# Two blocks of key weights loaded together through GpSimd's queue, with a new order of the head, in a two-layer linear-attention and MLP kernel

## The chip, the cores and the metric

The kernel runs on one core of one Trainium2 chip. The core has five engines that run side by side, each through its own list of instructions, in order: TensorE (PE, matrix products; PEld is its weight loads), VectorE (DVE), ScalarE (ACT), GpSimd (POOL) and SyncE (SP). SP, ACT and POOL can also issue DMAs; all DMAs run on the core's 16 DMA engines. The metric is the device time of one execution in microseconds. Times inside the profile count from the start of the profiled span.

## What is computed

`x` is 2048 tokens of 512 numbers in bf16. Two kinds of blocks alternate, A, B, A, B, each behind a layer norm and with a residual:

```python
def _A_ref(x, wqkv, wo):
    qkv = (x @ wqkv).reshape(B, S, 3, H, Dh)...      # H = 32, Dh = 16
    phi = lambda t: jnp.where(t > 0, t + 1, jnp.exp(t)) + 1e-6
    pq, pk = phi(q), phi(k)
    kv = jnp.einsum("bhsd,bhse->bhde", pk, v)
    z = jnp.einsum("bhsd->bhd", pk)
    num = jnp.einsum("bhqd,bhde->bhqe", pq, kv)
    den = jnp.einsum("bhqd,bhd->bhq", pq, z)[..., None] + 1e-6
    return (num / den)... @ wo

def _B_ref(x, w1, b1, w2, b2):
    y = _layernorm(x, axis=-1)
    h = _gelu(jnp.einsum("bsd,df->bsf", y, w1) + b1)                 # F = 1792
    return jnp.einsum("bsf,fd->bsd", h, w2) + b2

x = x + _A_ref(_layernorm(x, axis=-1), A_wqkv, A_wo)
x = x + _B_ref(_layernorm(x, axis=-1), B_w1, B_b1, B_w2, B_b2)
x = x + _A_ref(_layernorm(x, axis=-1), A_wqkv, A_wo)
x = x + _B_ref(_layernorm(x, axis=-1), B_w1, B_b1, B_w2, B_b2)
```

Linear attention needs the sum over all tokens of `pk` times `v` before any output: a first pass over the tokens builds that sum, a second one uses it.

## The kernel before, in words

**Tiles.** The tokens are cut into four chunks of 512 (c = 0 to 3) and each chunk into four row tiles of 128 (st = 4c + k). The 512 features are four blocks of 128. Weights stay in the on-chip memory once loaded: `wqkv` (queries, keys, values side by side, four feature blocks each), `wo`, `w1`, `w2`.

**The first pass (the head).** For each row tile of the first block A: statistics of the layer norm on VectorE (statsA0_st, aggrA0_st, L775 and L777), the reciprocal root on GpSimd (vepsA0_st at L782, powA0_st at L784), the normed row tile (normA0_st, L803 on VectorE or L798 on ScalarE), a transpose (TA0_st), the key product (K0_st, L879: one matmul for each of the four feature blocks), the key's `phi` (expk0_st at L847, reluk0_st at L858, mink0_st and phik0_st on VectorE, L860 and L864), and the product that sums `pk` times the normed tile over all row tiles (G0_st, L984, held in four PSUM banks). The sum of `pk` (Z0_c, L970) and the queries (Q0_c_k, L896 and L909) run in between. Values are never formed for each token: the sum is multiplied with the value weights at the end (KV0, L1034).

The first tiles take short cuts. Row tiles 0 and 1 are only centred (cenA0_st, L789), transposed on PE (PTC0, PTC1 at L825, brought back by ACT as tcC0, tcC1 at L835), and scaled later, inside the exponential and the relu of their keys. Tiles 2 and 3 are normed and transposed on PE too (PTA0_2, PTA0_3, tcA0_2, tcA0_3). Tile 3's statistics are made by ACT (sumA0_3 at L766, sqA0_3 at L770, with negA0_3 on GpSimd between them). All other transposes are DMAs on SP's queue (L812). The key product of tile 0 is cut into parts, so that each waits only for the key blocks it reads: `"ks0": "2|0|3|1"` makes four parts of one matmul (K0_0a to K0_0d), which read blocks 2, 0, 3 and 1 in that order.

Before that work, while nothing has been loaded, PE runs 15 matmuls on a constant whose result nobody reads (warm0 to warm8, L749).

**The loads at the start.** `LOADS` (L243) lists them: name, queue, what, chunk or 0, first and last block, and what must be done first. x0 is the first row tile of chunk 0, x1 the other three, xc1 to xc3 the other chunks of `x` (512 KB each), wq the query weights (512 KB), and wka, wkb, wkc, wkd one key block each (128 KB). SP issues x0, x1, wka, wkc, then xc1 (which waits until x0 has landed), wq, xc3, and later xc2 among its transposes; ACT issues wkb (behind `ones`, a VectorE memset) and wkd. The remaining weights (wv, wo, w1, w2) are issued by GpSimd much later, at L728, when all first transposes are issued.

GpSimd starts with small constants: id0 and id1 (the unit matrix `idp`, L719 and L720, read by the PE transposes), neghalf (L722), and bdm0 and bdm1 (the block-diagonal mask, L731 and L734, the first of which needs `ones`).

**The order.** The program is built as a graph of named operations. Nothing is scheduled at run time or at build time: `ORDER` holds the full list of operations of each engine, written out, and `PLACES` the buffer each tile lives in. `Settled.run` (L144) takes the lists as they are, and `assign_waits` (L186) puts the semaphore waits that the graph needs before each operation. So an operation that waits holds up all that stand behind it on its engine.

**The rest.** After KV0 and the products M0, the second pass makes outputs of block A (WO0, L1123), the MLP (W10 at L1153, gelu at L1158, W20 at L1190) and, chunk by chunk, the first pass of the next block A. The last layer writes the output from L1202 and L1184.

Of the kernel before, what the change touches and what calls it, by code (L numbers as in the profile page):

```python
# [185 lines left out]
def assign_waits(graph, order, sems, dma_sems):  # L186
# [1173 lines left out]
```

## Time and profile before

| What | us |
|---|---|
| median of 3 runs | 323.23 (323.01 to 323.62) |
| the profiled execution | 323.1, with a span of 321.9 |
| first matmul of useful work (PTC0) | starts 4.61 |
| x0 lands | 3.23 |
| xc1 issued, landed | 3.24, 8.07 |
| PE's last idle time over 0.1 us before the tail (0.47) | ends 9.16 |
| PE busy | 318.0 of 321.9 |
| last matmuls (L1176) | 316.70 to 319.92 |

In the views of the trace that follow, a row of the chain in order of time has a start, a length and what ran. A row of the timeline has a start, a length, the engine, the line of the kernel, the operation, what it writes and reads with sizes, and in brackets how long its engine had been idle before it and what ended that. Lengths of PE rows are a little longer than what they hold back, since matmuls overlap: eight 512-column matmuls that start 0.216 us apart show as 1.89 us on the timeline. The granted clock of the core was 1.00.

### The profile page before, as it was taken

To read this page: it belongs to the slowest core of one execution; us is meant where nothing else is said; L and a number is where in the kernel's file an instruction comes from. 1 tells how busy PE (TensorE), PEld (TensorE's weight loads), DVE (VectorE), ACT (ScalarE), POOL (GpSimd) and SP (SyncE) were. 2 spreads that over 40 slices of the span, in tenths; PEclk is the share of its full clock that TensorE was granted. 3 is DMA by queue.
4 is the path that set the end of the run, shared out by engine and by line. 5 is a ranking of instruction groups with operands and counts; after the bars stand their busy time and mean duration, and the time that the engine had idled before them with its cause. 6 is when DMAs were issued, how large, how long until landed. Compare 5 with 4: busy or idle time off the path is not lost.

```text
span 321.9 us, 4748 instructions
## 1 busy us (share of the span) xinstructions
PE 318.0 (99%) x1703; PEld 157.4 (49%) x1703; DVE 218.1 (68%) x529; ACT 189.3 (59%) x324; POOL 145.5 (45%) x216
## 2 busy tenths in 40 slices
PE   8999999999999999999999999999999999999997
PEld 3444554666444444444444444558544444444444
DVE  5998789999786774028848899999889881101103
ACT  5898656797730636667962367979634442663320
POOL 6573978688655355101822415887454163000000
DMA  7844793142121412111010200122232322201002
GB/s 257 200 81 85 241 348 85 35 82 36 33 49 34 82 33 51 34 33 32 18 40 10 51 16 0 35 51 52 50 62 54 98 65 67 49 0 35 16 33 65
DMA packets 52355, 21.68 MB, mean 67 GB/s; under 512 B 47532, under 2 KB 50860, under 8 KB 52332
## 3 DMA queue, kind: packets, MB, share of 16 engines
q1 hardware_dynamic: 50844, 16.37, 22.4%
q0 software_dynamic: 1056, 4.72, 4.3%
q10 hardware_dynamic: 432, 0.30, 0.3%
q8 instruction: 13, 0.21, 0.3%
q14 instruction: 10, 0.08, 0.1%
HBM read 8.00 MB, written 2.10 MB: 31 GB/s over the span
## 4 chain that ended last, share of the span: by engine, by line
PE 97%; DMA 2%; DVE 0%; issue 0%
PE ps L1153 30%; PE ps L1190 29%; PE ps L1123 9%; PE ps L879 8%; PE ps L896 6%; PE ps L984 4%; PE ps L1013 4%; DMA t<-in_A_x_dram 2%; PE ps L909 2%; PE ps L1176 1%; PE ps L970 1%; PE ps L1034 1%; PE ps L1057 1%; PE ps L1100 1%; DVE stats L775 0%; PE ps L1048 0%
## 5 line engine op out<-in xcount | busy, mean ns | idle before, releaser
L1158 ACT ACTIVATE gT<-ps,b1c 128x512 bf16<-128x512 f32 (+1 forms) x140 | 77.0, 601 | 68.7 <-PE ps L1153 68.1
L1153 PE MATMUL ps<-t,w 128*128 128x512 bf16 (+1 forms) x560 | 102.5, 336 | 0.0
L1190 PE MATMUL ps<-w,gT 128*128 128x512 bf16 x434 | 98.6, 379 | 0.0
L1153 PEld LDWEIGHTS ps<-t,w 128*128 128x128 bf16 x560 | 54.8, 98 | 43.7 <-ACT gT L1158 0.2
L1190 PEld LDWEIGHTS ps<-w,gT 128*128 128x128 bf16 x434 | 42.5, 98 | 50.4
L784 POOL TENSOR_TENSOR rstd<-veps,neghalf 128x1 f32<-128x1 f32 x64 | 39.0, 625 | 41.1 <-DVE veps L782 38.9
L847 ACT ACTIVATE eb<-ps 128x512 bf16<-128x512 f32 x62 | 35.4, 606 | 19.3 <-PE ps L896 7.3
L1200 DVE TENSOR_TENSOR yb<-ps,xsb 128x512 bf16<-128x512 f32 x15 | 10.2, 688 | 41.4 <-PE ps L1190 41.4
L775 DVE BATCH_NORM_STATS2 stats<-xsb 128x6 f32<-128x512 f32 x48 | 32.0, 681 | 0.3
L1123 PE MATMUL ps<-gtb,t 128*128 128x512 bf16 x128 | 31.4, 379 | 0.0
L879 PE MATMUL ps<-wqkv,t 128*128 128x512 bf16 x128 | 30.9, 379 | 0.3 <-ACT t L835 0.3
L858 ACT ACTIVATE rb<-ps 128x512 bf16<-128x512 f32 x43 | 25.3, 607 | 5.8 <-PE ps L879 5.8
L798 ACT ACTIVATE yb<-xsb,nmr,rstd 128x512 bf16<-128x512 f32 x21 | 16.9, 814 | 15.1 <-POOL nmr L795 15.1
L896 PE MATMUL ps<-wqkv,t 128*128 128x512 bf16 x96 | 24.1, 379 | 0.0
L1089 POOL TENSOR_TENSOR t<-t,rr 128x512 bf16<-128x512 bf16 x18 | 19.3, 1072 | 9.0 <-DVE rr L1085 6.4
L782 POOL TENSOR_SCALAR veps<-mv 128x1 f32<-128x1 f32 x35 | 8.2, 236 | 32.7 <-DVE mv L777 31.3
L1196 DVE TENSOR_TENSOR xsb<-ps,xsb 128x512 f32<-128x512 f32 x16 | 10.8, 678 | 17.9 <-PE ps L1190 17.9
L1139 POOL TENSOR_TENSOR xsb<-xsb,b2b 128x512 f32<-128x512 f32 x17 | 21.4, 1267 | 3.0 <-DVE yb L803 2.9
L1077 POOL TENSOR_TENSOR lr<-t,zrow 128x512 f32<-128x512 bf16 x14 | 16.5, 1179 | 7.3 <-ACT zrow L997 4.5
L1123 PEld LDWEIGHTS ps<-gtb,t 128*128 128x128 bf16 x128 | 12.5, 98 | 14.5
L803 DVE TENSOR_SCALAR yb<-xsb,mv,rstd 128x512 bf16<-128x512 f32 x27 | 14.5, 542 | 7.3 <-POOL rstd L784 6.0
L879 PEld LDWEIGHTS ps<-wqkv,t 128*128 128x128 bf16 x128 | 12.1, 98 | 14.7 <-ACT t L835 0.9
(99 smaller groups left out, 363.7 us busy)
## 6 DMA issues: line engine op xcount, KB each, us to landing
w<-in_B_w_dram POOLq DMA_DIRECT2D x4, 896.0 KB, 9.1
out_dram<-yb SPq DMA_DIRECT2D x15, 128.0 KB, 2.0
t<-in_A_x_dram SPq DMA_DIRECT2D x3, 512.0 KB, 4.8
t<-yb SPq DMA_TRANSPOSE x62, 2.5
wqkv<-in_A_wqkv_dram SPq DMA_DIRECT2D x1, 512.0 KB, 5.9
wqkv<-in_A_wqkv_dram POOLq DMA_DIRECT2D x1, 512.0 KB, 4.7
wo<-in_A_wo_dram POOLq DMA_DIRECT2D x1, 512.0 KB, 5.3
t<-in_A_x_dram SPq DMA_DIRECT2D x1, 384.0 KB, 3.3
```

Source lines behind the costliest of these rows:

```text
L775: G.op("dve", lambda e: e.bn_stats(stats[:, s.slot, :], src()), 620, reads=src_keys, writes=[k + "s"], tiles=[s, *src_tiles], name=f"stats ...
L784: G.op("pool", lambda e: e.tensor_tensor(rstd[:, s.slot:s.slot + 1], veps[:, s.slot:s.slot + 1], neghalf[:], op=ALU.pow), 570, reads=[k + ...
L847: G.op("act", lambda e: e.activation(eb[:, et.slot, :], bank(bt), ACT.Exp, scale=by()), 478, reads=[src_key, *more_keys], writes=[f"e{tag} ...
L858: G.op("act", lambda e: e.activation(rb[:, rt.slot, :], bank(bt), ACT.Relu, scale=by()), 478, reads=[src_key, *more_keys], writes=[f"r{tag ...
L879: ins = e.matmul(bank(b), lhsT=yTa(yT)[:, dt, k * P:(k + 1) * P], rhs=wqkv[:, dt, D:2 * D], start=(i == 0 and n == 0), stop=(i == len(part ...
L896: ins = e.matmul(bank(b), lhsT=yTa(yT)[:, dt, k * P:(k + 1) * P], rhs=wqkv[:, dt, 0:D], start=(dt == 0), stop=(dt == DT - 1))
L1089: lambda e, d=d, tok=tok, heads=heads: e.tensor_tensor(heads(tok()), heads(tok()), rr[:, d.slot, :].unsqueeze(2).broadcast_to([P, H, DH]), ...
L1123: ins = e.matmul(bank(wb), lhsT=yTa(pq)[:, kt, k * P:(k + 1) * P], rhs=gtb[:, kt, :], start=(kt == 0), stop=(kt == DT - 1))
L1139: G.op("pool" if on_pool else "dve", lambda e: e.tensor_tensor(xsb[:, st, :], xsb[:, st, :], b2b[:], op=ALU.add), 1120 if on_pool else 600 ...
L1153: ins = e.matmul(bank(b, n), lhsT=w1[:, dt, ft * P:(ft + 1) * P], rhs=yTa(yT)[:, dt, k0 * P:k1 * P], start=(dt == 0), stop=(dt == DT - 1))
L1158: G.op("act", lambda e, ft=ft, b=b, k0=k0, k1=k1, n=n: e.activation(gT[:, g.slot, ft * 512 + k0 * P:ft * 512 + k1 * P], bank(b, n), ACT.Ge ...
L1190: ins = e.matmul(bank(b), lhsT=gT[:, g.slot, ft * 512 + k * P:ft * 512 + (k + 1) * P], rhs=w2[:, ft, :], start=(ft == 0), stop=(ft == FT - 1))
```

## The change

Five things change in the tables, and several functions get options that this kernel's tables leave unused.

1. Key blocks 2 and 3 came by ACT's queue (wkb, wkd), blocks 0 and 1 by SP's (wka, wkc). Now blocks 2 and 3 come together in one load of 256 KB, wkp, issued by GpSimd; ACT's wkb carries block 0 and SP's wka block 1, and wkc and wkd no longer exist.
2. GpSimd's list starts id0, neghalf, id1, bdm0, bdm1, wkp instead of id0, neghalf, bdm0, bdm1, id1; wkp waits for nothing but its turn.
3. The key product of tile 0 is cut into three parts, block 0, block 1, and blocks 2 and 3 together. K0_0d no longer exists; K0_0c has two matmuls and waits for wkp.
4. The orders of all five engines in the head (and, with small differences, on to the second pass) and the places of many tiles are new. G0_0 now stands ahead of K0_3 on PE. On VectorE, mink0_0 moves ahead of normA0_1, and normA0_5 moves behind phik0_1. On GpSimd wv, wo and w1 move apart, with phik0_8 between wv and wo and phiq0_1_1 between wo and w1. One of the warm matmul groups moves from behind PTC0 to ahead of it.
5. A few operations change their engine: pr0_3_1, pr0_3_3, b20_2 and nine of the small veps operations swap between VectorE and GpSimd.

```diff
-    LOADS=[['x0', 'sp', 'x', 0, 0, 1, ''], ['x1', 'sp', 'x', 0, 1, 4, ''], ['wkb', 'act', 'wk', 0, 2, 3, 'ones'], ['wka', 'sp', 'wk', 0, 0, 1, ''], ['wkd', 'act', 'wk', 0, 3, 4, ''], ['wkc', 'sp', 'wk', 0, 1, 2, ''], ['xc1', 'sp', 'x', 1, 0, 4, 'x0'], ['wq', 'sp', 'wq', 0, 0, 4, ''], ['xc3', 'sp', 'x', 3, 0, 4, ''], ['xc2', 'sp', 'x', 2, 0, 4, '']],
+    LOADS=[['x0', 'sp', 'x', 0, 0, 1, ''], ['x1', 'sp', 'x', 0, 1, 4, ''], ['wkb', 'act', 'wk', 0, 0, 1, 'ones'], ['wka', 'sp', 'wk', 0, 1, 2, ''], ['wkp', 'pool', 'wk', 0, 2, 4, ''], ['xc1', 'sp', 'x', 1, 0, 4, 'x0'], ['wq', 'sp', 'wq', 0, 0, 4, ''], ['xc3', 'sp', 'x', 3, 0, 4, ''], ['xc2', 'sp', 'x', 2, 0, 4, '']],
+    CHUNKS=[[0, 1, 2, 3], [0, 1, 2, 3], [0, 1, 2, 3]],
...
         "sp":
-            "x0 x1 wka wkc xc1 wq xc3 TA0_0 TA0_1 xc2 TA0_5 TA0_4 TA0_7 TA0_6 TA0_13 TA0_14 TA0_15 TA0_12 TA0_8 TA0_10 TA0_9 "
+            "x0 x1 wka xc1 wq xc3 TA0_0 TA0_1 xc2 TA0_5 TA0_4 TA0_7 TA0_6 TA0_13 TA0_14 TA0_12 TA0_8 TA0_15 TA0_10 TA0_9 "
...
         "pe":
-            "warm0 warm8 warm2 warm6 PTC0 warm1 warm7 warm5 warm4 warm3 K0_0a K0_0b PTC1 K0_0c K0_0d PTA0_2 K0_1 PTA0_3 K0_2 "
-            "K0_3 G0_0_0 G0_1_0 Q0_0_2 Q0_0_1 Q0_0_0 K0_5 G0_2_0 K0_4 Z0_0 G0_3_0 Q0_1_0 K0_7 Q0_1_3 K0_6 G0_4_0 G0_5_0 "
+            "warm0 warm1 warm6 warm8 warm4 PTC0 warm2 warm5 warm7 K0_0a warm3 K0_0b PTC1 K0_0c PTA0_2 K0_1 PTA0_3 K0_2 G0_0_0 "
+            "K0_3 G0_1_0 Q0_0_1 Q0_0_2 Q0_0_0 K0_5 G0_2_0 Q0_1_0 K0_4 K0_7 G0_3_0 Q0_1_3 G0_4_0 Z0_0 K0_6 Q0_1_2 G0_5_0 K0_14 "
...
         "act":
-            "wkb wkd sumA0_3 tcC0 sqA0_3 tcC1 reluk0_0 tcA0_2 expk0_0 tcA0_3 expk0_1 reluk0_1 reluk0_3 expk0_2 reluk0_2 "
+            "wkb sumA0_3 tcC0 sqA0_3 tcC1 expk0_0 tcA0_2 reluk0_0 expk0_1 tcA0_3 reluk0_1 expk0_2 reluk0_3 reluk0_2 expk0_3 "
...
         "dve":
-            "ones statsA0_0 aggrA0_0 cenA0_0 statsA0_2 statsA0_1 aggrA0_2 aggrA0_1 cenA0_1 normA0_0 vepsA0_1 normA0_2 "
-            "statsA0_5 normA0_3 aggrA0_5 normA0_1 statsA0_4 mink0_0 aggrA0_4 phik0_0 mink0_1 normA0_5 phik0_1 statsA0_7 "
+            "ones statsA0_0 aggrA0_0 cenA0_0 statsA0_2 statsA0_1 aggrA0_2 aggrA0_1 cenA0_1 normA0_0 normA0_2 vepsA0_1 "
+            "statsA0_5 normA0_3 mink0_0 normA0_1 phik0_0 aggrA0_5 statsA0_4 mink0_1 aggrA0_4 phik0_1 normA0_5 statsA0_7 "
...
         "pool":
-            "id0 neghalf bdm0 bdm1 id1 vepsA0_0 powA0_0 negA0_3 vepsA0_2 powA0_2 vepsA0_3 powA0_3 powA0_1 vepsA0_5 powA0_5 "
...
-            "nmrA0_10 vepsA0_9 powA0_9 nmrA0_11 phik0_14 eps6 wv wo phik0_8 w1_0 w1_1 w2_0 w2_1 phiq0_1_1 pr0_0_0 pz0_1_0 "
+            "id0 neghalf id1 bdm0 bdm1 wkp vepsA0_0 powA0_0 negA0_3 vepsA0_2 powA0_2 vepsA0_3 powA0_3 powA0_1 b1z vepsA0_5 "
...
+            "vepsA0_10 powA0_10 vepsA0_9 nmrA0_10 nmrA0_11 powA0_9 phik0_14 wv phik0_8 wo phiq0_1_1 w1_0 w1_1 w2_0 w2_1 "
...
-        "den0_3": "tok", "den1_1": "tok", "den1_2": "tok", "den1_3": "tok", "ks0": "2|0|3|1", "normA0_0": "dve",
+        "den0_3": "tok", "den1_1": "tok", "den1_2": "tok", "den1_3": "tok", "ks0": "0|1|23", "normA0_0": "dve",
```

The options that stay unused are a load of half a row tile (`load_half`), queries of half a chunk in the other layout (`by_half`), and another order of the chunks: `CHUNKS` keeps 0, 1, 2, 3 in each pass, so `attn_z`, `attn_g_held`, `attn_g_chunk`, `attn_out` and `mlp_up` build the same operations as before with a flag for the first or last chunk in place of a comparison with 0 or 3.

More of the change, by code (lines that the diff above doesn't have):

```diff
@@ L709, in load_w, with load_half @@
                                [f"{which}_{d}" for d in range(d0, d1)], name=name, kb=128 * (d1 - d0), after=after)
+        def load_half(name, queue, h, after):
+            G.parts[("x0", 0)] = (("x0", 0, 0), ("x0", 0, 1))
+            ps_ = slice(64 * h, 64 * h + 64)
+            loaded[name] = dma(queue, lambda e: e.dma_start(
+                t4[ps_, x0[0].slot, 0:D].rearrange("p (k d) -> p k d", k=1), rows(x_dram, 0)[ps_, 0:1, :]),
+                [("x0", 0, h)], [x0[0]], name=name, kb=64, after=after)
         for name, queue, what, at, lo, hi, behind in cf["LOADS"]:
             after = [loaded[b] for b in behind.split()]
-            if what == "x":
+            if what == "half":
+                load_half(name, queue, at, after)
+            elif what == "x":
                 load_x(name, queue, at, lo, hi, after)
@@ L751, in build_kernel, with by_token, by_half @@
             G.op("pe", warm, sum(cols) / 1.2, tiles=[wu], name=f"warm{n}", n=len(cols))
-        def by_token(L, c):
-            return eng(f"den{L}_{c}") == "tok"
+        def by_token(L, c, k=0):
+            way = eng(f"den{L}_{c}")
+            return way == "tok" or (way == "half" and k >= 2)
+        def by_half(L, c):
+            return eng(f"den{L}_{c}") == "half"
+        tokq = {}
         def norm(src, src_keys, src_tiles, double, on_act, tag, src16=False, head=False, centred=None):
@@ L854, in phi @@
                                                              op0=ALU.add, op1=ALU.max),
-                     600, reads=[f"e{tag}", src_key], writes=[dst_key], tiles=[et, bt, *dst_tiles], name=f"phi{tag}", lat=90)
+                     600 if n == D else 330, reads=[f"e{tag}", src_key], writes=[dst_key], tiles=[et, bt, *dst_tiles], name=f"phi{tag}", lat=90)
                 return
             rt = Tile(RB, f"r{tag}")
-            G.op("act", lambda e: e.activation(rb[:, rt.slot, :], bank(bt), ACT.Relu, scale=by()), 478, reads=[src_key, *more_keys],
+            G.op("act", lambda e: e.activation(rb[:, rt.slot, 0:n], bank(bt, n), ACT.Relu, scale=by()), 478 if n == D else 265, reads=[src_key, *more_keys],
@@ L887, in attn_q, with fn @@
         def attn_q(L, c, yT, pq):
-            if by_token(L, c):
-                for k in range(4):
+            half = by_half(L, c)
+            own = pq
+            if half:
+                own = tokq[(L, c)] = Tile(T4, f"pqt{L}_{c}")
+            n = 2 * P if half else 4 * P
+            if not by_token(L, c):
+                for kt in range(DT):
+                    b = Tile(psum, f"q{L}_{c}_{kt}" + "c" * half, "q")
+                    def fn(e, kt=kt, b=b):
+                        for dt in range(DT):
+                            ins = e.matmul(bank(b, n), lhsT=wqkv[:, dt, kt * P:(kt + 1) * P], rhs=yTa(yT)[:, dt, 0:n],
+                                           start=(dt == 0), stop=(dt == DT - 1))
+                        return ins
+                    G.op("pe", fn, 4 * MM if n == D else 4 * (n / 2.4 + 2.5), reads=[f"yT{L}_{4 * c + k}" for k in range(n // P)] + ["wq"], writes=[f"q{L}_{c}_{kt}" + "c" * half],
+                         tiles=[b, yT], name=f"Q{L}_{c}_{kt}" + "c" * half, lat=MM_DRAIN, n=4)
+                    phi(b, f"q{L}_{c}_{kt}" + "c" * half, lambda kt=kt: yTa(pq)[:, kt, 0:n], f"pq{L}_{c}_{kt}" + "c" * half, [pq], f"q{L}_{c}_{kt}" + "c" * half, n=n)
+            for k in range(4):
+                if by_token(L, c, k):
                     b = Tile(psum, f"q{L}_{c}_{k}", "q")
@@ L900, in attn_q, with attn_z @@
                          tiles=[b, yT], name=f"Q{L}_{c}_{k}", lat=MM_DRAIN, n=4)
-                    phi(b, f"q{L}_{c}_{k}", lambda k=k: t4[:, pq.slot, k * D:(k + 1) * D], f"pq{L}_{c}_{k}", [pq],
+                    phi(b, f"q{L}_{c}_{k}", lambda k=k: t4[:, own.slot, k * D:(k + 1) * D], f"pq{L}_{c}_{k}", [own],
                         f"q{L}_{c}_{k}")
-                return
-            for kt in range(DT):
-                b = Tile(psum, f"q{L}_{c}_{kt}", "q")
-                def fn(e, kt=kt, b=b):
-                    for dt in range(DT):
-                        ins = e.matmul(bank(b), lhsT=wqkv[:, dt, kt * P:(kt + 1) * P], rhs=yTa(yT)[:, dt, :],
-                                       start=(dt == 0), stop=(dt == DT - 1))
-                    return ins
-                G.op("pe", fn, 4 * MM, reads=[f"yT{L}_{4 * c + k}" for k in range(4)] + ["wq"], writes=[f"q{L}_{c}_{kt}"],
-                     tiles=[b, yT], name=f"Q{L}_{c}_{kt}", lat=MM_DRAIN, n=4)
-                phi(b, f"q{L}_{c}_{kt}", lambda kt=kt: yTa(pq)[:, kt, :], f"pq{L}_{c}_{kt}", [pq], f"q{L}_{c}_{kt}")
         zfirst = {}
-        def attn_z(L, c, pks):
-            by_sum = [int(v) for v in (eng("zc0") or "").split()] if L == 0 else list(range(NC - 1))
+        def attn_z(L, c, pks, order):
+            by_sum = [int(v) for v in (eng("zc0") or "").split()] if L == 0 else order[:NC - 1]
+            others = [v for v in order if v not in by_sum]
             def fold(add):
@@ L973, in attn_z, with attn_g_held @@
             G.op("pe", fn, 400, reads=[f"pk{L}_{4 * c + k}" for k in range(4)] + ["onesm"], writes=[f"zc{L}_{c}"], tiles=[b, *pks], name=f"Z{L}_{c}", lat=MM_DRAIN, n=16)
-            total(b, f"zc{L}_{c}", f"zs{L}_{c}", bool(L) or c != min(v for v in range(NC) if v not in by_sum))
-            if L == 0 and by_sum and c == max(v for v in range(NC) if v not in by_sum):
+            total(b, f"zc{L}_{c}", f"zs{L}_{c}", bool(L) or c != others[0])
+            if L == 0 and by_sum and c == others[-1]:
                 fold(True)
-        def attn_g_held(L, st, k, y, ykey, pk, gb):
-            parts = [(dc,) for dc in range(DT)] if st == ST - 1 else [tuple(range(DT))]
+        def attn_g_held(L, st, k, y, ykey, pk, gb, first, last):
+            parts = [(dc,) for dc in range(DT)] if last else [tuple(range(DT))]
             for part in parts:
@@ L984, in fn @@
                         ins = e.matmul(ps[:, gb.slot + dc, :], lhsT=yb[:, y.slot, dc * P:(dc + 1) * P], rhs=pkb[:, pk.slot, :],
-                                       start=(st == 0), stop=(st == ST - 1))
+                                       start=first, stop=last)
                     return ins
                 keys = [f"g{L}_{dc}" for dc in part]
-                G.op("pe", fn, len(part) * MM, reads=[ykey, f"pk{L}_{st}"] + (keys if st else []), writes=keys,
+                G.op("pe", fn, len(part) * MM, reads=[ykey, f"pk{L}_{st}"] + ([] if first else keys), writes=keys,
                      tiles=[y, pk, gb], name=f"G{L}_{st}_{part[0]}", lat=MM_DRAIN, n=len(part))
@@ L1004, in attn_g_out, with attn_g_chunk @@
                 copy(gtb[:, dc, :], gb, f"g{L}_{dc}", ("gt", dc), dc % 2, f"g{L}_{dc}", off=dc)
-        def attn_g_chunk(L, c, ys, ykeys, pks):
+        def attn_g_chunk(L, c, ys, ykeys, pks, first, last):
             for dc in range(DT):
@@ L1042, in attn_kv @@
                  reads=["zs", "bdmask"], writes=["zb"], name=f"zb{L}", lat=40, fast=True)
-            if any(by_token(L, c) for c in range(NC)):
+            if any(by_token(L, c, 3) for c in range(NC)):
                 zr = Tile(psum, f"zr{L}", "t")
@@ new lines, in attn_den @@
+            half = by_half(L, c)
+            src = tokq[(L, c)] if half else pq
+            pt = pq if half or not by_token(L, c) else Tile(T4, f"pt{L}_{c}")
+            n = 2 * P if half else 4 * P
+            if not by_token(L, c):
+                for kt in range(DT):
+                    tag = f"{L}_{c}_{kt}" + "c" * half
+                    b = Tile(psum, f"d{tag}", "n")
+                    r = Tile(LR, f"lr{tag}")
+                    key = f"pq{L}_{c}_{kt}" + "c" * half
+                    G.op("pe", lambda e, kt=kt, b=b: e.matmul(bank(b, n), lhsT=zb[:, kt * P:(kt + 1) * P], rhs=yTa(pq)[:, kt, 0:n], start=True, stop=True),
+                         MM if n == D else n / 2.4 + 2.5, reads=[key, "zb"], writes=[f"d{tag}"], tiles=[b, pq], name=f"D{tag}", lat=MM_DRAIN)
+                    G.op("act", lambda e, b=b, r=r: e.activation(lr[:, r.slot, 0:n], bank(b, n), ACT.Ln, bias=eps6[:]), 575 if n == D else 362,
+                         reads=[f"d{tag}", "eps6"], writes=[f"l{tag}"], tiles=[b, r], name=f"ln{tag}", lat=90, table="exp")
+                    G.op("act", lambda e, r=r: e.activation(lr[:, r.slot, 0:n], lr[:, r.slot, 0:n], ACT.Exp, scale=-1.0), 536 if n == D else 323,
+                         reads=[f"l{tag}"], writes=[f"l{tag}"], tiles=[r], name=f"rec{tag}", lat=110, table="exp")
@@ L1093, in attn_den @@
-                    dma("sp", lambda e, k=k, tok=tok: e.dma_start_transpose(yTa(pt)[:, :, k * P:(k + 1) * P], tok()), [f"pt{tag}"],
-                        tiles=[pq, pt], reads=[f"pq{tag}"], name=f"TP{tag}", sem=("pT", pq, k), transpose=True)
-                return pt
-            for kt in range(DT):
-                b = Tile(psum, f"d{L}_{c}_{kt}", "n")
-                r = Tile(LR, f"lr{L}_{c}_{kt}")
-                tag = f"{L}_{c}_{kt}"
-                G.op("pe", lambda e, kt=kt, b=b: e.matmul(bank(b), lhsT=zb[:, kt * P:(kt + 1) * P], rhs=yTa(pq)[:, kt, :], start=True, stop=True),
-                     MM, reads=[f"pq{tag}", "zb"], writes=[f"d{tag}"], tiles=[b, pq], name=f"D{tag}", lat=MM_DRAIN)
-                G.op("act", lambda e, b=b, r=r: e.activation(lr[:, r.slot, :], bank(b), ACT.Ln, bias=eps6[:]), 575,
-                     reads=[f"d{tag}", "eps6"], writes=[f"l{tag}"], tiles=[b, r], name=f"ln{tag}", lat=90, table="exp")
-                G.op("act", lambda e, r=r: e.activation(lr[:, r.slot, :], lr[:, r.slot, :], ACT.Exp, scale=-1.0), 536,
-                     reads=[f"l{tag}"], writes=[f"l{tag}"], tiles=[r], name=f"rec{tag}", lat=110, table="exp")
+                         lambda e, kt=kt, r=r: e.tensor_tensor(yTa(pq)[:, kt, 0:n], yTa(pq)[:, kt, 0:n], lr[:, r.slot, 0:n], op=ALU.mult),
@@ new lines, in attn_den, with tok, heads @@
+                         (1150 if on_pool else 600) if n == D else (580 if on_pool else 330),
+                         reads=[f"l{tag}", key], writes=[key], tiles=[r, pq], name=f"pr{tag}", lat=40,
+                         fast=not on_pool)
+            for k in range(4):
+                if not by_token(L, c, k):
+                    continue
+                tag = f"{L}_{c}_{k}"
+                r = Tile(LR, f"lr{tag}")
+                d = Tile(RD, f"rd{tag}")
+                def tok(k=k):
+                    return t4[:, src.slot, k * D:(k + 1) * D]
+                def heads(ap):
+                    return ap.rearrange("p (h x) -> p h x", x=DH)
+                on_pool = eng(f"pz{tag}") != "dve"
+                G.op("pool" if on_pool else "dve",
+                     lambda e, r=r, tok=tok: e.tensor_tensor(lr[:, r.slot, :], tok(), zrow[:], op=ALU.mult), 1150 if on_pool else 600,
+                     reads=[f"pq{tag}", "zrow"], writes=[f"l{tag}"], tiles=[r, src], name=f"pz{tag}", lat=60,
+                     fast=not on_pool)
+                G.op("dve", lambda e, r=r, d=d, heads=heads: e.tensor_reduce(rd[:, d.slot, :], heads(lr[:, r.slot, :]),
+                                                                              mybir.AxisListType.X, ALU.add), 600,
+                     reads=[f"l{tag}"], writes=[f"rd{tag}"], tiles=[r, d], name=f"red{tag}", lat=60)
+                G.op("dve", lambda e, d=d: e.tensor_scalar(rd[:, d.slot, :], rd[:, d.slot, :], 1e-6, None, op0=ALU.add), 100,
+                     reads=[f"rd{tag}"], writes=[f"rd{tag}"], tiles=[d], name=f"den{tag}", lat=60)
+                G.op("dve", lambda e, d=d: e.reciprocal(rr[:, d.slot, :], rd[:, d.slot, :]), 300,
+                     reads=[f"rd{tag}"], writes=[f"rr{tag}"], tiles=[d], name=f"rec{tag}", lat=60)
@@ new lines, in attn_den, with attn_out @@
+                     1150 if on_pool else 600, reads=[f"rr{tag}", f"pq{tag}"], writes=[f"pq{tag}"], tiles=[d, src],
+                     name=f"pr{tag}", lat=60, fast=not on_pool)
+                dma("sp", lambda e, k=k, tok=tok: e.dma_start_transpose(yTa(pt)[:, :, k * P:(k + 1) * P], tok()), [f"pt{tag}"],
+                    tiles=[src, pt], reads=[f"pq{tag}"], name=f"TP{tag}", sem=("pT", src, k), transpose=True)
+            return pt
+        def attn_out(L, c, k, pq, base, base_keys, base_tiles, first):
@@ L1116, in attn_out @@
             st = 4 * c + k
             wb = Tile(psum, f"wo{L}_{st}", "w")
-            parts = [(kt,) for kt in range(DT)] if st == 0 else [tuple(range(DT))]
+            parts = [(kt,) for kt in range(DT)] if first else [tuple(range(DT))]
             for part in parts:
@@ L1124, in wfn @@
                     return ins
-                G.op("pe", wfn, len(part) * MM, reads=([f"pt{L}_{c}_{k}"] if by_token(L, c) else [f"pq{L}_{c}_{kt}" for kt in part]) + [("gt", kt) for kt in part]
+                G.op("pe", wfn, len(part) * MM, reads=([f"pt{L}_{c}_{k}"] if by_token(L, c, k) else [f"pq{L}_{c}_{kt}" + "c" * by_half(L, c) for kt in part]) + [("gt", kt) for kt in part]
                      + ([f"wo{L}_{st}"] if part[0] else []), writes=[f"wo{L}_{st}"], tiles=[wb, pq],
@@ L1141, in mlp_front, with mlp_up @@
                  fast=not on_pool)
-        def mlp_up(L, c, yT, g):
-            parts = [(0, 2), (2, 4)] if c == 0 else [(0, 4)]
+        def mlp_up(L, c, yT, g, first):
+            parts = [(0, 2), (2, 4)] if first else [(0, 4)]
             for hf, (k0, k1) in enumerate(parts):
@@ L1206, in build_kernel @@
         gb = Tile(psum, "g4", "g4", 4)
-        pq1, trs = [], []
-        for c in range(NC):
+        pq1, trs = {}, []
+        orders = cf["CHUNKS"]
+        for c in orders[0]:
             yT = Tile(T4, f"yT0_{c}")
             pq = Tile(T4, f"pq0_{c}")
-            pq1.append(pq)
+            pq1[c] = pq
             pks = []
@@ L1252, in build_kernel @@
         for L in range(2):
-            nxt = []
-            for c in range(NC):
+            nxt = {}
+            chunks = orders[1 + L]
+            for c in chunks:
                 yT = Tile(T4, f"yBT{L}_{c}")
```

69 lines of the change are left out of this document (20 added, 49 removed), and 309 rows, old and new, of tables (ORDER, PLACES, WAY).

## The prediction

> **What bounds the kernel now.** I read the page first (engine rows, chain that ended last), then the chain in order of time, then the timeline of the first 13 us, then the rows of the loads.
>
> ```profile
> PE 318.0 (99%) x1703; PEld 157.4 (49%) x1703; DVE 218.1 (68%) x529; ACT 189.3 (59%) x324; POOL 145.5 (45%) x216
> PE 97%; DMA 2%; DVE 0%; issue 0%
> ```
>
> TensorE (PE) sets the end. The chain in order of time says from where on (start, length, what):
>
> ```profile
> 3.24 4.83 DMA t<-in_A_x_dram
> 8.07 0.02 issue
> 8.09 0.69 DVE stats L775
> 8.79 0.33 DVE yb L803
> 9.12 0.04 issue
> 9.16 0.40 PE ps L825 x4
> 9.56 1.73 PE ps L879 x8
> 11.28 1.73 PE ps L984 x8
> ```
>
> From 9.16 us on the chain is PE alone, at 0.216 us for a 512-column matmul (1.73/8), to its last group near 320 us. So a change of the head (the work before the dense part) can only move the moment from which PE is dense, or put a hole into what is dense now. That moment hangs on xc1, which lands at 8.07: VectorE's statsA0_5 waits for it and stands ahead of normA0_3, whose transpose PTA0_3 is the 9.16 row. The timeline shows the rest of the head (start, length, engine; idle before it):
>
> ```profile
> 3.25 0.29 POOL L720 TENSOR_SCALAR_AFFINE_SELECT idp<-idp 128x128 bf16<-128x128 bf16 x1
> 4.25 0.34 POOL L782 TENSOR_SCALAR veps<-mv 128x1 f32<-128x1 f32 x1 [0.71 <-DVE mv L777]
> 6.78 0.59 PE L879 MATMUL ps<-wqkv,t 128*128 128x512 bf16 x2
> 7.48 0.68 ACT L858 ACTIVATE rb<-ps,rstd 128x512 bf16<-128x512 f32 x1
> 8.05 0.60 ACT L835 ACTIVATE t<-ps 128x512 bf16<-128x512 bf16 x1
> 8.53 0.70 ACT L847 ACTIVATE eb<-ps,rstd 128x512 bf16<-128x512 f32 x1
> 9.16 0.40 PE L825 MATMUL ps<-idp,yb 128*128 128x128 bf16 x4 [0.47 <-DVE yb L803]
> 10.32 0.43 DVE L864 TENSOR_TENSOR pkb<-eb,rb 128x512 bf16<-128x512 bf16 x1
> ```
>
> The 6.78 row is K0_0's second pair, the one that needs the last two key blocks; it follows PTC1 without a wait, so all four blocks are there by then and none of them binds today. The four loads, SP's and ACT's, took 3.5 us at least from issue to landing:
>
> ```profile
> DMA to landing us min/median/max: 3.5/4.0/5.9
> L728 POOL DMA_DIRECT2D wqkv<-in_A_wqkv_dram x1: 974/974/974, 32.5 to 32.5; - x1
> wqkv<-in_A_wqkv_dram POOLq DMA_DIRECT2D x1, 512.0 KB, 4.7
> 35.20:36.20 1.00, 1.00 (x20) 1.00 0.97 401
> ```
>
> The first line is that of the loads at L708 (5.9 is the 512 KB wq); the next two are wv, the first load that GpSimd (POOL) issues: 0.97 us of POOL, 4.7 us to landing for 512 KB. The last (a table by stage: busy PE, clock, DMA share, GB/s) is the rate at which wv flows, 401 GB/s; in the 1 us stage before it, 34.2 to 35.2, that table has 86.
>
> **The change part by part.** *Removed issues.* ACT issues one key load fewer (0.45 us) and SP one fewer (0.43): nothing. ACT's next work waits for x1 until 4.60, and SP's next issue, xc1, waits for x0 until 3.24.
>
> *The issue on POOL.* wkp follows the second mask (2.46 + 0.85); idp's select, 0.29 us, moves ahead of both masks, where POOL stood idle 0.50 us for ones. So wkp issues where idp's row is now, 3.25, and ends at 4.22 by wv's 0.97. The next operation, vepsA0_0, starts at 4.25 because of VectorE: nothing, covered by that row's 0.71 us of idle time. Were the issue 0.3 longer, rstd of row tile 0 would be 0.3 late, and negA0_3 behind it with sqA0_3 and tcC1 on ACT.
>
> *The landing.* K0_0c (the second pair, blocks 2 and 3) now waits for wkp alone, and PTA0_2, K0_1, PTA0_3 and K0_2 stand behind it on PE. No row shows a 256 KB load of POOL's queue in the head. Bounds from the nearest rows: 3.5 us (a 128 KB block in the same stretch; 6.75) and 5.9 (the 512 KB wq in that stretch; 9.15). The nearest row is wv, same queue, same 1 KB rows: 4.7 less 256 KB at 401 GB/s (0.65) is 4.05, a landing at 7.30. Two corrections work against each other: in the head xc1 and wq share the engines, and at half the rate 0.65 is added (7.95); and wv's slow first microsecond (86 GB/s) came after a stretch with idle DMA engines, while the head runs at 350 to 420, which may save up to 1.0. I take 7.40, range 6.75 to 9.15.
>
> [...]
>
> *From landing to dense.* With T the landing: K0_0c starts at T+0.05. ACT comes 0.70 after such a pair starts (6.78 to 7.48): expk0_0 at T+0.75. ACT's start-to-start times are 0.57 after a scaled activation and 0.48 after a copy (7.48, 8.05, 8.53), so tcA0_2 is at T+1.32 and reluk0_0 at T+1.80, done at T+2.48. phik0_0 on VectorE (0.43, with 0.07 to hand over) is done at T+2.98, and G0_0, 0.08 later, at T+3.06. In the new order G0_0 stands ahead of K0_3, right behind K0_2. Where nothing is late K0_2 starts at 9.39 as now and takes 0.86, so G0_0 is due at 10.26. Break-even is T = 7.20. K0_2 itself is looser: 2 matmuls (0.43), PTA0_2 (0.23), K0_1 (0.86), PTA0_3 (0.23) put it at T+1.81, and with tcA0_2 at T+1.97, due 9.39, so T = 7.42. Beyond 7.20 each microsecond of landing is a microsecond of time.
>
> *Orders of the head.* The number of matmuls stays, and the dense part has no hole to close, so they gain nothing behind 9.16; they cost if something arrives after its turn. The case with the least room: normA0_5 moves behind phik0_0 and phik0_1 (11.01 now, near T+4.7 = 12.1 then), its transpose TA0_5 takes 2.5 us by the median of its group and lands near 14.7 if nothing is queued ahead, and K0_5 is due 2.59 behind Q0's start at 12.85, at 15.44: hidden by 0.7 us, less where xc2's 512 KB stand ahead in SP's queue. wv's and wo's issues get one GpSimd operation (1.15) more between them, w1's another; wv landed at 37.2 and KV0 reads it at 46.78, w1's first use is at 60.62: nothing.
>
> *Sum.* The profiled execution took 323.1 us (span 321.9). T - 7.20 = +0.2: 323.3. The median of the runs is 0.13 above that execution, so 323.4 for the median: no change that can be told (0.2%, 0.65 us, is about what a measurement of this kernel can tell).
>
> **The rivals.** *The load is early and the head gains.* K0_0c cannot start before PTC1 is through, 6.78, so T counts as 6.75 at the least and G0_0 starts at 9.81 instead of 10.26: -0.45, 322.8. For it speaks that two key blocks no longer run ahead of xc1 in SP's and ACT's queues. It needs xc1 at 7.55 instead of 8.07, or statsA0_5 still holds PTA0_3 at 9.16. This is the largest gain that I find, and it is still within 0.2%.
>
> *The load is late: slower.* wkp is issued last of the head's first loads, and meets xc1 (512 KB), wq (512) and xc3 (512) on the same DMA engines. wq took 5.9 us there. At 5.0 us, between wv's 4.05 and wq's 5.9, it lands at 8.25: +1.05, 324.3; at 5.9 it is +1.95, 325.2. It decides from T = 7.85 on (+0.65). Against it: wq is twice as large and stands behind xc1 in one queue, wkp is alone in its own. [...]
>
> *A hole further on.* Were TA0_5 0.5 us later than K0_5's turn, or another transpose as late, PE would stand for that 0.5 on top of the +0.2: 324.0. For it: ten of the head's VectorE operations change places. Against it: all of them hang on T, as PE's own order does, so they are late together.
>
> **How the numbers follow.** The forecast (T between 7.0 and 7.85) has 0.50; the early landing 0.13; the late one 0.27; a hole further on 0.10. The early landing gives a gain of over 0.2% only where run-to-run scatter helps it, and I leave something for a gain that I don't see: 0.06 faster. Slower by over 0.2%: all of the late case and 0.07 of the hole's, 0.34. Within 0.2%: 0.60. The range runs from the first rival less 0.1 of scatter, 322.7, to a landing near 8.5 (+1.3), 324.6; 9.15 is left out.
>
> **What would show it.** K0_0's second pair should start at the landing of wkp, near 7.4, with PE idle before it and that DMA as the releaser. POOL's wkp row at 3.25, 0.9 to 1.0 us, with vepsA0_0 at 4.25. xc1 landing before 8.07. G0_0 near 10.4, ahead of K0_3. Behind it PE without a hole, and the whole span longer by what G0_0 or Q0's first matmul (12.85 now) is late. Wrong it would be if K0_0c waits for nothing, if it waits beyond 7.85, or if PE shows holes of 0.3 us and more behind 13 us.

## The result and the profile after

| | median us | runs | range | ratio to the kernel before (95% interval) |
|---|---|---|---|---|
| before | 323.42 | 4 | 323.01 to 323.62 | |
| after | 328.07 | 4 | 325.69 to 329.37 | 1.0138 (1.0092 to 1.0185) |
| after, again, beside other kernels | 326.82 | 4 | 324.79 to 327.53 | 1.0106 (1.0069 to 1.0143) |

The first two rows are one measurement; in the third, the kernel before had 322.97 beside it (7 runs). So the change costs 4.7 us in the one and 3.9 in the other. The kernel now scatters by 3.7 and 2.7 us over four runs, the one before by 0.6 here, though 35 later runs of it lie between 322.51 and 325.29. A run that is over 1.5% longer than the fastest of its kernel counts as slow and is left out of the ratios; that befell two runs, both of e2 below. The profiled execution took 328.55 us, with a span of 327.3. PE's busy share in 40 slices, before:

```profile
PE   8999999999999999999999999999999999999997
```

and the page after: engine rows first, then PE's busy share and granted clock in the slices (a 9 is 90% or more), then the chain that ended last:

```profile
PE 317.8 (97%) x1673; PEld 158.5 (48%) x1703; DVE 219.6 (67%) x531; ACT 188.6 (58%) x324; POOL 144.0 (44%) x215
...
PE   6599999999999999999999999999999999999997
...
PEclk9799999999999999999999999999999999999999
...
PE 95%; DMA 3%; DVE 1%; issue 1%; POOL 1%
```

PE's work is the same (30 matmul records are missing from this trace), but the span is 5.4 us longer. All of that is in the first two slices, 0 to 16 us: there PE is busy for 6 and 5 tenths, where it had 8 and 9, and in the second of them its clock is below full (7 tenths). Behind them the slices read as before. The chain of waits in order of time, 2 to 17 us (start, length, what), says what released PE:

```profile
2.45 0.79 POOL bdmask L745
3.24 8.26 DMA wqkv<-in_A_wqkv_dram
11.51 0.05 issue
11.55 1.03 PE ps L896 x2
12.59 0.43 PE ps L842 x4
13.01 1.71 PE ps L896 x4
14.72 0.34 PE ps L842 x4
15.06 0.86 PE ps L896 x4
15.92 0.86 PE ps L1006 x4
```

Before, xc1 (3.24 to 8.07) stood in this place. Now it is wkp, and it takes 8.26 us from its issue to its landing. The rows that answer to those of before, on the timeline:

```profile
3.24 0.92 POOL L710 DMA_DIRECT2D wqkv<-in_A_wqkv_dram  x1
...
4.25 0.33 POOL L799 TENSOR_SCALAR veps<-mv 128x1 f32<-128x1 f32 x1
...
6.61 0.40 PE L842 MATMUL ps<-idp,yb 128*128 128x128 bf16 x4
...
11.55 1.03 PE L896 MATMUL ps<-wqkv,t 128*128 128x512 bf16 x2 [4.54 <-DMA wqkv<-in_A_wqkv_dram]
...
12.62 0.69 ACT L864 ACTIVATE eb<-ps,rstd 128x512 bf16<-128x512 f32 x1 [4.98 <-PE ps L896]
...
14.40 0.43 DVE L881 TENSOR_TENSOR pkb<-eb,rb 128x512 bf16<-128x512 bf16 x1 [0.45 <-ACT rb L875]
...
15.76 1.03 PE L1006 MATMUL ps<-pkb,yb 128*128 128x512 bf16 x4
```

The issue on GpSimd (first row) and the operation behind it (second) stand where the prediction had them. PTC1 (third) is through at 7.0; then PE is idle for 4.54 us in front of K0_0c. The last row is G0_0, at 15.76 where the prediction had it due at 10.26: 5.50 us late, and the execution is 328.55 - 323.1 = 5.45 us longer. So the whole loss is in hand by 15.76.

One thing in these rows the landing does not explain. K0_0c's two matmuls show as 1.03 us, and the same two took 0.59 before. The table by stage (length, busy time of PE, PEld, DVE, ACT and POOL, then granted clock, DMA share, GB/s) shows why:

```profile
10.00:11.00 1.00, 0.00 (x0) 0.00 (x0) 0.00 (x0) 0.00 (x0) 0.00 (x0) 1.00 0.73 140
11.00:12.00 1.00, 0.45 (x2) 0.18 (x3) 0.00 (x0) 0.00 (x0) 0.00 (x0) 0.71 0.32 33
12.00:13.00 1.00, 1.00 (x7) 0.68 (x6) 0.00 (x0) 0.38 (x1) 0.00 (x0) 0.50 0.02 4
...
14.00:15.00 1.00, 1.00 (x7) 0.64 (x6) 0.59 (x3) 0.62 (x2) 0.00 (x0) 0.58 0.00 0
15.00:16.00 1.00, 1.00 (x8) 0.41 (x5) 0.86 (x3) 1.00 (x3) 0.79 (x3) 1.00 0.65 131
```

From 11.42 (0.29 of a stage at 11 to 12 is 0.58 us at half clock) to 14.84 the clock is 0.50. That is a stretch of 3.4 us, just when PE has work again.

### The profile page after: what moved, and what is told of

Read it like the earlier page. It is cut to its first block, busy times and chain, and to the rows that moved or that the text cites. A ratio compares the mean times of both kernels' runs of the same rounds, so it can differ in the third digit from the quotient of the medians.

```text
span 327.3 us, 4713 instructions
## 1 busy us (share of the span) xinstructions
PE 317.8 (97%) x1673; PEld 158.5 (48%) x1703; DVE 219.6 (67%) x531; ACT 188.6 (58%) x324; POOL 144.0 (44%) x215
## 4 chain that ended last, share of the span: by engine, by line
PE 95%; DMA 3%; DVE 1%; issue 1%; POOL 1%
PE ps L1180 30%; PE ps L1217 28%; PE ps L896 9%; PE ps L1150 8%; PE ps L929 6%; PE ps L1006 4%; PE ps L1035 4%; DMA wqkv<-in_A_wqkv_dram 3%; PE ps L917 2%; PE ps L1203 1%; PE ps L1056 1%; PE ps L992 1%; PE ps L1079 1%; DVE gacc L1044 0%; PE ps L1095 0%
## 5 line engine op out<-in xcount | busy, mean ns | idle before, releaser
L1180 PE MATMUL ps<-t,w 128*128 128x512 bf16 (+1 forms) x553 | 101.8, 336 | 0.4
L1180 PEld LDWEIGHTS ps<-t,w 128*128 128x128 bf16 x560 | 54.8, 98 | 43.7
L801 POOL TENSOR_TENSOR rstd<-veps,neghalf 128x1 f32<-128x1 f32 x64 | 38.0, 612 | 36.9 <-DVE veps L799 34.8
L877 DVE TENSOR_SCALAR eb<-eb 128x512 bf16<-128x512 bf16 x45 | 14.3, 322 | 11.1 <-ACT eb L864 10.9
L1166 POOL TENSOR_TENSOR xsb<-xsb,b2b 128x512 f32<-128x512 f32 x16 | 20.2, 1271 | 2.9 <-DVE yb L820 2.9
```

Source lines behind the costliest of these rows:

```text
L801: G.op("pool", lambda e: e.tensor_tensor(rstd[:, s.slot:s.slot + 1], veps[:, s.slot:s.slot + 1], neghalf[:], op=ALU.pow), 570, reads=[k + ...
L1166: G.op("pool" if on_pool else "dve", lambda e: e.tensor_tensor(xsb[:, st, :], xsb[:, st, :], b2b[:], op=ALU.add), 1120 if on_pool else 600 ...
L1180: ins = e.matmul(bank(b, n), lhsT=w1[:, dt, ft * P:(ft + 1) * P], rhs=yTa(yT)[:, dt, k0 * P:k1 * P], start=(dt == 0), stop=(dt == DT - 1))
```

## The experiments

Four theories were set against each other. Q: the 1.5 MB that SP's queue has under way (xc1, wq, xc3) hold wkp up. S: a load of GpSimd's queue is this slow in the head by itself. O: the new orders cost something themselves. G: a part of the loss is the clock that falls to half behind PE's idle time, not the idle time itself. Each kernel below is the changed kernel with one edit; a diff shows its main line, and the engines' lists follow it.

**The orders without the load (e1).** Block 2 goes back to ACT's queue and block 3 to SP's; GpSimd loads no keys. The new orders and K0_0c with two matmuls stay.

```diff
-['wkp', 'pool', 'wk', 0, 2, 4, '']
+['wkd', 'act', 'wk', 0, 2, 3, ''], ['wkc', 'sp', 'wk', 0, 3, 4, '']
```

> The changed kernel with key block 2 on ACT's queue and block 3 on SP's, as single loads, and nothing of the first loads on GpSimd; all new orders kept. If GpSimd's load is the whole cost (theory Q or S below), K0_0c waits for nothing, PE is dense from 9.2 us or earlier, and the time is 322.8 to 323.7. If the new orders cost something themselves (theory O), it stays above 325. Theory Q: the backlog of SP's queue (xc1, wq, xc3, 1.5 MB) starves the load. Theory S: GpSimd's path is slow in the head by itself, whatever else is in flight.

Measured: 323.09 us beside 323.63 for the kernel before, ratio 0.9985 (0.9969 to 1.0001). A second time:

> The kernel with the new orders and all four key blocks on the hardware queues, a second time. Its G0_0 stood at 10.24, where the prediction has the kernel before: ratio 0.998 to 1.000, at most 0.5 us faster.

Measured: 323.31 beside 323.34, ratio 0.9994 (0.9980 to 1.0007). G0_0 stood at 10.24 in the first profile. Theory O falls: the orders alone make no difference that can be told, and the whole loss belongs to the load.

**The same load at the same moment on ACT's queue (e2).**

```diff
-['wkp', 'pool', 'wk', 0, 2, 4, '']
+['wkp', 'act', 'wk', 0, 2, 4, 'x0']
```

> The same 256 KB load at the same moment (behind x0's landing, about 3.25 us), but issued by ACT: a queue of its own, the same backlog on SP. Theory Q: it lands as late, 9.5 us or later, and the time is above 325. Theory S: it lands at 6.5 to 7.7 and the time is 322.9 to 323.8.

Measured: 324.27 us (10 runs, 323.31 to 329.25), ratio 1.0023 (0.9998 to 1.0047). In the profiled execution, which took 329.0, the load was issued at 3.27, its packets began at 5.05, and it took 6.2 us from issue to landing (T, the landing, 9.43), where this queue's first key block took 3.5. So this load can be late on ACT's queue too, and two further runs, 326.35 and 326.39, have the lowered clock (0.995) that the changed kernel has when it is late. Both theories missed: the landing of the profile is all but Q's 9.5, the median lies between S's 323.8 and Q's 325. But with the same load, moment and company, ACT's queue costs 0.2%, and GpSimd's 1.4% and 1.1% in the two measurements of the changed kernel, with intervals that do not meet. Over all ten runs the mean is 1.7 us above the kernel before, against 4.4 and 3.4 for the changed kernel. The two were not run beside each other, only each beside the kernel before; by these numbers the queue has a share in the loss that the company alone does not explain, and why is not shown.

**The load first on GpSimd's queue (e3, e9).** wkp is issued ahead of id1 and the two masks, at 1.36 instead of 3.24.

```diff
-"id0 neghalf id1 bdm0 bdm1 wkp vepsA0_0 ..."
+"id0 neghalf wkp id1 bdm0 bdm1 vepsA0_0 ..."
```

> wkp still on GpSimd, but ahead of both masks, issued near 1.05 us instead of 3.24. Theory Q: it is in flight before SP's backlog (xc1's first packets come after 4 us), lands by 7.0, and the time is 322.8 to 323.7. Theory S with a fixed 8 us from issue to landing: it lands near 9.3, PE waits 2.5 us, time about 325.5 to 326.

Measured: 323.00 us beside 323.63, ratio 0.9982 (0.9963 to 1.0001). The landing is 4.5 us behind the issue, T = 5.8, and the time is within Q's 322.8 to 323.7. From the timeline, K0_0's second pair, G0_0, and the first MLP product (L1180):

```profile
6.87 0.59 PE L896 MATMUL ps<-wqkv,t 128*128 128x512 bf16 x2
...
9.82 1.04 PE L1006 MATMUL ps<-pkb,yb 128*128 128x512 bf16 x4
...
60.88 5.85 PE L1180 MATMUL ps<-t,w 128*128 128x256 bf16 x52 [0.57 <-DMA t<-yb]
```

K0_0c waits for nothing, and G0_0 is 0.44 earlier than due, but that execution took 323.49: PE gives 0.57 back 50 us later, where a transpose is late for the first MLP product. A second time:

> The kernel with wkp issued first on GpSimd's queue, a second time and with more rounds, for its place against the kernel before. The sum of the prediction with T near 5.9 and xc1 at 7.1: G0_0 at 9.8 instead of 10.26, 0.45 earlier, ratio 0.9986 or 0.3 to 0.6 us faster, if no hole opens behind; where the wait for a transpose ahead of the first W10 product stands again (0.6 us near 60 us in its first profile), no change.

Measured: 323.20 beside 323.34, ratio 1.0005 (0.9987 to 1.0024). Its profiled execution had G0_0 at 9.60, no such wait, and 322.5 us; one of its 12 runs took 325.49. The 0.44 and 0.66 us at the head are there, but no gain can be told in the medians. Issued 1.9 us earlier, the same load on the same queue is in time.

**What is under way beside it (e4, e8, e5).** The edit is a wait, one for each kernel, so that SP issues a load, and what stands behind it in its list, only when wkp has landed: in e4 wq and xc3, in e8 xc3, in e5 xc1, wq and xc3.

```diff
-['wq', 'sp', 'wq', 0, 0, 4, '']
+['wq', 'sp', 'wq', 0, 0, 4, 'wkp']
...
-['xc3', 'sp', 'x', 3, 0, 4, '']
+['xc3', 'sp', 'x', 3, 0, 4, 'wkp']
...
-['xc1', 'sp', 'x', 1, 0, 4, 'x0']
+['xc1', 'sp', 'x', 1, 0, 4, 'x0 wkp']
```

> wkp as in the change, but SP issues wq (and xc3 behind it) only when wkp has landed, so that only xc1 is in flight beside it. Theory Q: wkp lands at 7.0 to 8.2. Theory S: it lands at 10 or later, as in the change (11.5). The time is not the point here, since wq comes later too; by Q below 325.5, by S above 328.

> The changed kernel, but xc3 (and what stands behind it on SP's queue) is issued only when wkp has landed; xc1 and wq are as they were. If it is wq that holds wkp up (it is in flight when wkp's first packets go), wkp lands where it did, 9.5 to 11.5, and the time is 326 to 328 or more. If it is xc3, whose 4 KB packets run while wkp's last four engines are late, wkp lands at 8.0 to 9.0 and the time is 324 to 325.

> The changed kernel, but xc1 (and wq, xc3 behind it) is issued only when wkp has landed, so that no SP load runs beside it but x1 and wka. Theory Q: wkp lands 3.5 to 4.2 us after its issue, by 7.5, and PE does not wait for it; xc1 then lands near 12, holds statsA0_5 and PTA0_3 up, and the time is 326 to 328 for that other reason. Theory S: wkp still takes over 6 us, and the time is over 329.

Measured: e4 325.11 us, ratio 1.0045 (1.0025 to 1.0065); e8 325.48, 1.0069 (1.0045 to 1.0093); e5 325.89, 1.0087 (1.0054 to 1.0121). What they tell lies in the landings, the last number of the rows of the DMA issues (issue to landing). In the order e5, e4, e8:

```profile
wqkv<-in_A_wqkv_dram POOLq DMA_DIRECT2D x1, 256.0 KB, 3.5
```

```profile
wqkv<-in_A_wqkv_dram POOLq DMA_DIRECT2D x1, 256.0 KB, 4.2
```

```profile
wqkv<-in_A_wqkv_dram POOLq DMA_DIRECT2D x1, 256.0 KB, 6.1
```

and the changed kernel, whose three profiles (the first, e7 below, and e6 below, which leaves the loads as they are) have 8.3, 7.2 and 7.0:

```profile
wqkv<-in_A_wqkv_dram POOLq DMA_DIRECT2D x1, 256.0 KB, 8.3
```

The second column is from the trace's records of single packets (those of 4 KB on GpSimd's queue).

| issued while wkp is under way | wkp's packets, first to last start | landing behind the issue | T |
|---|---|---|---|
| nothing of 512 KB (e5) | 4.88 to 6.17 | 3.5 | 6.72 |
| xc1 (e4) | 5.65 to 6.86 | 4.2 | 7.42 |
| xc1, wq (e8) | 6.26 to 8.79 | 6.1 | 9.31 |
| xc1, wq, xc3 (changed kernel, first profile) | 6.67 to 10.84 | 8.3 | 11.51 |

Each 512 KB of SP's queue added: 0.7 us, then 1.9, then about 1 to 2. Each row is one execution, and the changed kernel's own three differ by 1.3 us; but e8's 6.1 lies below all three, and e4 and e5 far below. So Q holds on GpSimd's queue (e4's landing and time are what it expected), and S falls as it was put: left alone (e5), GpSimd's load took the 3.5 us of a block half its size on SP's or ACT's queue. What e2 left open, that the same company costs less on ACT's queue, is not settled by this. xc1 mostly delayed the load's start (by 0.77 us, with the packets' starts spread over 1.21 us beside 1.29), wq and xc3 stretched it (to 2.53 us with wq, 4.17 with both). e8 lies between its two expectations in landing and time, since wq and xc3 each have a share; of e5's two times 326.53 is within Q's 326 to 328 and 325.25 below it, and xc1 landed at 9.87 in the profile, not near 12.

None of the three repairs the time: in e8 the load still lands at 9.31, and in e4 and e5 what waits for it is needed too. The chain of e4:

```profile
3.24 4.18 DMA wqkv<-in_A_wqkv_dram
...
9.18 0.59 ACT rb L875
9.77 3.96 DMA t<-yb
13.73 0.05 issue
13.78 1.25 PE ps L917 x5
```

T is 7.42 and K0_0c starts 0.05 later, as good as on time; now the transposes, which stand behind wq and xc3 in SP's list, start to be issued at 8.42 instead of 6.84, and Q0 (L917), which waits for one, starts at 13.78 instead of 12.85. 323.1 + 0.93 = 324.0; that execution took 324.19.

**The wait filled (e6), beside the changed kernel (e7).** Fourteen matmuls on the constant, whose results nobody reads (warm9, with a PSUM buffer of its own), stand between PTC1 and K0_0c.

```diff
-WARM=[[512, 512, 512, 512, 512, 512, 512], [256], ...
+WARM=[[512, 512, 512, 512, 512, 512, 512], [256], ..., [512] * 14],
...
-PTC1 K0_0c PTA0_2
+PTC1 warm9 K0_0c PTA0_2
```

> The changed kernel with 14 more 512-column matmuls on the constant between PTC1 and K0_0c, so that PE works through its wait for wkp until about 10.0 us; the load and the rest are unchanged, and the 14 results are read by nobody. Theory G (the clock): a part of the loss is PE at half clock for one or two stretches of 3.4 us behind the idle time, 1.7 us of time each. Then the granted clock stays at 1.000 in every execution, the 512-column matmuls behind the wait start 0.216 us apart, and the median falls to about 325.5 to 327 (323.4 plus T less 7.2, T between 9.5 and 11.5), 1 to 2 us below the changed kernel in the same batch. Theory I (idle time alone): the loss is the wait itself; the filling changes nothing, or adds up to 0.5 where the load lands before 10.0, about 328.

> The changed kernel itself, beside the others on the same chip. Theories Q and G: executions fall into groups by the granted clock, near 325.7 with none, 327.5 with one and 329.3 with two stretches of half clock; in the profiled one wkp lands between 9.5 and 11.6. Theory S: wkp lands at 11.5 again, whatever the other transfers do, and the times lie within 1 us of 328.

Measured: e6 326.19 us, ratio 1.0094 (1.0075 to 1.0113); e7 326.82, 1.0106 (1.0069 to 1.0143). The medians cannot be told apart; the profiles can. The timeline of e7:

```profile
10.45 0.61 PE L896 MATMUL ps<-wqkv,t 128*128 128x512 bf16 x2 [3.61 <-DMA wqkv<-in_A_wqkv_dram]
...
12.86 1.91 PE L896 MATMUL ps<-wqkv,t 128*128 128x512 bf16 x4
14.57 1.21 PE L1006 MATMUL ps<-pkb,yb 128*128 128x512 bf16 x4
```

and of e6, where these lines of the kernel are three further on and the first row is the filling:

```profile
6.67 3.22 PE L763 MATMUL ps<-const-bfloat16-1.0 128*128 128x512 bf16 x14
10.25 0.61 PE L899 MATMUL ps<-wqkv,t 128*128 128x512 bf16 x2 [0.36 <-DMA wqkv<-in_A_wqkv_dram]
...
12.13 1.04 PE L899 MATMUL ps<-wqkv,t 128*128 128x512 bf16 x4
13.16 1.04 PE L1009 MATMUL ps<-pkb,yb 128*128 128x512 bf16 x4
```

The load landed almost at the same time in both, 10.40 and 10.21. K0_2, four matmuls, takes 1.91 us in e7 and 1.04 in e6, and G0_0 comes 4.17 behind the landing in e7 and 2.95 in e6. So a stretch of half clock costs 1.2 us here, and theory G holds for that share. e7's landing and its times by the clock are as Q and G expected, not as S did (11.5 again). In all four runs of e6 the granted clock was 1.000; in e7 it was 1.000 once (324.79 us) and 0.995 three times (326.56 to 327.53). The gain of 1 to 2 us in the median that was expected of e6 did not come. The filling ends near 9.9, so it also holds K0_0c up in every execution whose load lands earlier; that the 324.79 was such a one is worked out (T of about 8.9 by the sum), not shown, as it has no profile.

## Why the prediction was wrong

**The step that failed is "The landing".** It took T = 7.40, within 6.75 to 9.15. Measured were 11.51, and 10.40 and 10.21 in the other two profiles. The price of the load by itself was about right: 3.5 us alone and 4.2 with xc1 beside it, where the prediction reckoned with 4.05. (That e4's T of 7.42 meets the 7.40 is chance: the 7.40 was meant for company of xc1 and wq.) Wrong was the correction for company. It gave 0.65 for sharing the engines and took 0.55 of it back because wv's slow first microsecond might not come again; wq and xc3 cost 2.8 to 4.1 us beyond the T that e4 shows. The upper bound was no bound either: wq's 5.9 us is the landing of a load that had one 512 KB load ahead of it in its own queue, while wkp started behind xc1 and then ran against both wq and xc3. The "late load" rival named exactly this meeting, with a chance of 0.27, and argued against it that wkp is "alone in its own" queue; its latest landing was 9.15. It is alone there, but the DMA engines were busy with other queues beside it: from 4 to 9 us the packets of SP's queue took 83.2% of the 16 engines' time and those of GpSimd's 14.0%, and the busy share was 0.89 to 1.12 in every microsecond.

In the trace of the changed kernel wkp has 16 reports on its semaphore: twelve came from 7.92 to 9.19, the last four from 10.24 to 11.51, and K0_0c started 0.05 behind the last. In e4, with wq and xc3 out of the way, all 16 came from 6.76 to 7.42. So what K0_0c waited for was the last of the 16, and a mean rate in GB/s hides how late that one is.

**A term was missing from the sum.** The prediction had "beyond 7.20 each microsecond of landing is a microsecond of time". With the clock at full speed that is right within 0.15 us (e6: 3.01 us of landing, 2.87 of time). It left out the clock: in the profile of the changed kernel it was 0.50 for 3.41 us behind PE's wait, and six of that kernel's eight runs show a granted clock below 1.000. The steps behind the landing, checked against four profiles (time = 323.1 plus what G0_0 is late against 10.26):

| | T | clock behind the wait | G0_0 | less T | by the sum | measured |
|---|---|---|---|---|---|---|
| predicted | 7.40 | full | 10.46 | 3.06 | 323.3 | |
| changed kernel | 11.51 | half | 15.76 | 4.25 | 328.6 | 328.55 |
| changed kernel, again (e7) | 10.40 | half | 14.57 | 4.17 | 327.4 | 327.53 |
| xc3 behind (e8) | 9.31 | half | 13.30 | 3.99 | 326.1 | 326.30 |
| wait filled (e6) | 10.21 | full | 13.16 | 2.95 | 326.0 | 325.97 |

So of the 5.45 us of the profiled execution 4.31 are the landing (11.51 less 7.20) and about 1.2 the clock.

**What held.** *The issue on POOL*: 3.24 to 4.16, 0.92 us, and vepsA0_0 at 4.25, covered. *From landing to dense*: 2.95 at full clock where 3.06 was reckoned; G0_0 stands ahead of K0_3 right behind K0_2, and it is what binds. *xc1*, foreseen before 8.07: it landed at 8.12 in the first profile, 6.94 in e7 and 7.22 in e6; the 8.07 of the kernel before and the 8.12 are each the last of 16 reports, 0.65 and 1.03 us behind the other 15. *Orders of the head*: neutral, by e1 and e10. *The early landing*: e3 and e9 made it happen, and G0_0 came 0.44 and 0.66 earlier, as that rival had it (0.45); no gain can be told in the medians. *A hole further on*: none in the changed kernel, but the profiles of e3 and e2 had one of 0.57 and 1.0 near 60 us.

## What to carry to other kernels

A small load that the next step needs at once should be under way before the large loads that nothing waits for yet: issued at 1.36 it landed at 5.8 here (e3), issued at 3.24 between xc1 and wq at 11.51. A queue of its own did not protect it (8.3 us from issue to landing beside xc1, wq and xc3, 3.5 without them), and GpSimd's queue suffered more from the same company than ACT's (1.4% and 1.1% of the time against 0.2%). Take its price with the same company beside it, not from a quiet stretch, and where the rows only show quiet ones, let the range reach to the time at which all the bytes beside it are through (xc3 landed at 12.18 here, wkp at 11.51). Where PE would stand as long as it stood here with the clock falling (1.77 to 4.54 us), add an estimate for the clock (1.0 to 1.3 us for a stretch, by the table above), and look at the granted clock of single executions when a kernel's runs scatter more than those of the one before.

## What the runs showed of the hardware

**Half clock came in stretches of 3.4 us, behind short waits too.** In the head of the traces in which the clock fell, it was granted as 0.5 for 3.41 us or for twice that (6.83 in the profile of e2), and then was full again; in the changed kernel its record starts at 4.60 and changes at 11.42 and 14.84, 6.83 and 3.41 us apart. It fell with an idle time of 4.54 us in the changed kernel, and also with one of 2.25 (e8) and one of 1.77 (e5); with the wait filled but for 0.36 us (e6) it stayed at 1.000 in all four runs. What went with every fall was little work of PE in the 3.41 us just ahead of it: 0.00 us in the changed kernel, 1.06 in e7, 1.39 in e2, 1.48 in e8 and 1.60 in e5. The 3.41 us before those had 1.82 us of work in the changed kernel and 1.78 in e7, and there the clock stayed full. In e2 the clock stayed at half for a second stretch behind one with 2.47 us of work at half clock; behind 2.73 (e8) it came back.

The fall does not come at the same time in each execution: 11.42 in the changed kernel, 11.50 in e7, 8.68 in e8. Whether it comes goes with the scatter of the times: of the changed kernel's eight runs the two fastest (324.79 and 325.69) show a granted clock of 1.000, the five from 326.56 to 328.55 one of 0.995, and the slowest (329.37) one of 0.990. What sets the length of a stretch and the moment of a fall is not shown.

**On GpSimd's queue the load's first packet came later beside another queue's loads.** wkp's packets started 1.64 us behind the issue with no 512 KB load under way (e5), 2.41 with xc1 (e4), 3.02 with xc1 and wq (e8) and 3.43 in the changed kernel. It is not the 512 KB loads alone: issued at 1.36 in e3, beside x0, x1, wka and wkb, the first packet came 2.89 us behind the issue. VectorE did the same work beside the issue in e5 (the centring at 4.16, in the changed kernel at 4.18), so that work does not make the difference between 1.64 and 3.43. On ACT's queue, with the same company, the first packet came 1.78 us behind the issue (e2, one profile). What in the path holds GpSimd's load was not tried.
